# First squares of V in a buffer outside the weights' ring, weight blocks handed out later, and a new planned order

## The chip, the cores and the metric

The kernel runs on one NeuronCore of a Trainium2 chip, as one program of five instruction streams: PE (TensorE, matmuls), DVE (VectorE), ACT (ScalarE), POOL (GpSimd) and SP (SyncE), which here only issues DMAs. The metric is the device time of one execution in microseconds (us). The profile covers one execution; its span runs from the first to the last instruction.

## The reference

Causal attention over 4 batches of 12 heads, 448 positions and 64 dimensions, and behind it a product of four weight matrices on all 1792 tokens.

```python
# _attn_ref(q, k, v), each (4, 12, 448, 64)
scores = scale * np.matmul(q, k.transpose(0, 1, 3, 2))
scores = np.where(mask, -1000000000.0, scores)
scores = scores - np.max(scores, axis=-1, keepdims=True)
attn = np.exp(scores)
attn = attn / (np.sum(attn, axis=-1, keepdims=True) + 1e-09)
return np.matmul(attn, v).astype(np.float32)
...
# _moe_ref(x, w1, w2, w3, w_out), x (1792, 768), d_ff 1024
a = x @ w1
b = x @ w2
h = a * b @ w3
return (h @ w_out).astype(np.float32)
```

The weights arrive as 64-bit numbers. The inputs are random, Q and K enlarged by about 7.5.

## The kernel before

**The steps.** W3 and W_out are multiplied into one matrix first ("w34", line 776, float32, 8 blocks m of 16 products each; W3 is turned on PE in line 764 and the results are evacuated in lines 783 and 784). Attention works on 24 pairs of heads, 6 to a batch. For each pair Q and K are loaded and turned (line 488), the scores are computed (line 571), DVE masks them and takes the maximum (line 588), ACT takes the exponential (line 592), and the probabilities are split into two float16 parts `ph`: the high part on DVE, ACT or POOL (lines 617, 619 and 621), the low part always on DVE (line 624). A transposing DMA brings them into `pt` and `ptt`, PE multiplies them with V (lines 644 and 649), and the result goes into `xt`, again in two parts (lines 658 to 661). The part `pht` (448 columns) is the last one that DVE makes of a pair.

**The gate.** For each batch `gate` multiplies `xt` with 16 weight blocks `w16` (even ones of W1, odd ones of W2; lines 900 to 902, three products for each of 6 pairs of heads d, so 18 to a block). `norms` (line 851) finds the batch's scale before the results can be stored. `project` multiplies the gated values with w34 (lines 960 to 962).

**Weights.** A weight block takes a DMA of 64-bit words, `decode` to float32 (ACT lines 677 and 679, DVE line 681, and the addition of line 684 on POOL or DVE), squares on ACT (line 392) for the scale, a tiny product on PE (line 405), three small DVE instructions (lines 408 to 413), and the two float16 parts (lines 716 to 720 and 723). The float32 values wait in one of three tiles of the ring `da`. A ring hands out its tiles in the order in which the code asks for them, so a user further down the code waits until the user three places earlier is finished with the tile. The squares of V (line 392, called by `take_v`), from which comes the scale of V, use a `da` tile only as a place for unwanted output. In the code `take_v` for batch 0 stands behind all of `w34`, and `w34` with `nf=3` asks for weight blocks 0 to 9 while it goes through m = 3 to 7.

**The order.** The whole program is recorded first as operations with a due time (`Program.add`). `Program.order` is a list scheduler: it simulates the engines with written-down costs and picks, for the engine that is free first, the ready operation with the earliest due time. Where an operation may run on several engines the first free one takes it. The due times come from the table PLAN. The engines then execute their instructions strictly in the recorded order, and SP issues its DMAs in order too.

## Time and profile before

| what | value |
|---|---|
| median of 3 runs | 583.81 us (582.77 to 598.71) |
| profiled execution, its own time | 582.41 us |
| its span, first to last instruction | 580.6 us |
| PE busy | 548.0 us (94% of the span) |
| DVE busy | 383.6 us (66%) |
| ACT busy | 325.2 us (56%) |
| POOL busy | 168.3 us (29%) |
| mean granted TensorE clock | 0.987 |

The table is an average over stages. It is read with a table by stage beside it, in which a stage's length less an engine's busy time is that engine's idle time there, and in which the granted clock tells how much of PE's busy time was spent at half speed.

### The profile page before, as it was taken

The numbers are of one execution on the slowest core, as the hardware profiler recorded it, in microseconds if no ns is written. First come the engines' busy times: TensorE is split into PE (matmuls) and PEld (weight loads), VectorE is DVE, ScalarE is ACT, GpSimd is POOL, SyncE is SP. The second block draws the span as 40 slices with busy tenths as digits, with TensorE's granted clock in tenths as the row PEclk, the third lists the DMA queues.
The fourth block names the chain that finished last, engine by engine and source line by source line (L and its number), as shares of the span: only waits on it lengthen the run. The fifth ranks groups of instructions, "written<-read, shape, count | busy, mean of one in ns | idle before, by whom it ended". The sixth has DMA issues, their size and how long they took to land.

```text
span 580.6 us, 10748 instructions
## 1 busy us (share of the span) xinstructions
PE 548.0 (94%) x3872; PEld 304.4 (52%) x3872; DVE 383.6 (66%) x1057; ACT 325.2 (56%) x764; POOL 168.3 (29%) x128
## 2 busy tenths in 40 slices
PE   3899999886888999999999999999999999999997
PEld 1465555553545555466545555565455566555564
DVE  5635989999897979983587969826897861211100
ACT  6856999877667676853366547534754541111111
POOL 3021674656434445140021533201333410000000
PEclk9999999999889999999999999999999999999999
DMA  8999887798689868676656887786647781000011
GB/s 318 340 255 214 242 206 212 230 198 172 118 162 183 164 145 141 121 147 165 120 112 127 160 145 132 178 193 124 137 94 122 114 175 51 0 1 1 15 42 54
DMA packets 224949, 84.59 MB, mean 146 GB/s; under 512 B 205952, under 2 KB 221824, under 8 KB 224896
## 3 DMA queue, kind: packets, MB, share of 16 engines
q1 hardware_dynamic: 224896, 83.91, 66.4%
q8 instruction: 30, 0.49, 0.4%
q14 instruction: 23, 0.19, 0.1%
HBM read 43.78 MB, written 5.51 MB: 85 GB/s over the span
## 4 chain that ended last, share of the span: by engine, by line
PE 63%; DVE 3%; ACT 1%; DMA 1%; issue 1%; POOL 0%; ACTq 0%; POOLq 0%; DVEq 0%
PE mm L900 8%; PE mm L902 7%; PE mm L901 7%; PE sc L571 6%; PE mm L960 4%; PE mm L962 4%; PE mm L961 4%; PE tr L900 4%; PE tr L901 4%; PE tr L902 4%; PE av L649 3%; PE tr L960 2%; PE tr L962 2%; PE tr L961 2%; PE av L644 1%; DMA qkt<-da 1%
## 5 line engine op out<-in xcount | busy, mean ns | idle before, releaser
L900 PE MATMUL mm<-xt,w 128*128 128x448 f16 x258 | 91.7, 355 | 0.0
L902 PE MATMUL mm<-xt,w 128*128 128x448 f16 x258 | 91.4, 354 | 0.0
L901 PE MATMUL mm<-xt,w 128*128 128x448 f16 x258 | 91.4, 354 | 0.0
L592 ACT ACTIVATE p<-p,mx 128x256 f32<-128x256 f32 (+2 forms) x144 | 71.6, 499 | 23.6 <-DVE mx L588 23.3
L776 PE MATMUL mm<-wof,w3t 128*128 128x384 f32 x192 | 71.1, 513 | 4.9 <-POOL wof L684 2.7
L621 POOL TENSOR_SCALAR ph<-p,rc 128x256 f16<-128x256 f32 (+2 forms) x48 | 47.0, 986 | 87.6 <-DVE rc L602 44.3
L624 DVE SCALAR_TENSOR_TENSOR ph<-p,rc,ph 128x384 f16<-128x384 f32 (+2 forms) x144 | 67.6, 517 | 2.5 <-ACT ph L619 2.2
L571 PE MATMUL sc<-qkt 64*128 64x384 f16 (+7 forms) x480 | 63.2, 365 | 4.0 <-DVE mx L588 3.8
L902 PEld LDWEIGHTS <-w 128*128 128x128 f16 x384 | 37.6, 98 | 40.7 <-issue 5.9
L900 PEld LDWEIGHTS <-w 128*128 128x128 f16 x384 | 37.6, 98 | 39.6 <-issue 7.7
L901 PEld LDWEIGHTS <-w 128*128 128x128 f16 x384 | 37.7, 98 | 31.0 <-issue 1.8
L776 PEld LDWEIGHTS mm<-wof,w3t 128*128 128x128 f32 x192 | 35.5, 197 | 29.7 <-issue 3.6
L960 PE MATMUL mm<-w34h,arena 128*128 128x384 f16 x152 | 49.6, 327 | 0.0
L962 PE MATMUL mm<-w34h,arena 128*128 128x384 f16 x152 | 49.5, 326 | 0.0
L961 PE MATMUL mm<-w34l,arena 128*128 128x384 f16 x152 | 49.5, 326 | 0.0
L901 PE MATMUL tr<-xt,w 128*128 128x448 f16 x126 | 44.6, 354 | 5.1 <-DVE xt L661 5.1
L900 PE MATMUL tr<-xt,w 128*128 128x448 f16 x126 | 44.5, 353 | 0.8 <-ACT at L911 0.5
L902 PE MATMUL tr<-xt,w 128*128 128x448 f16 x126 | 44.6, 354 | 0.0
L422 POOL TENSOR_SCALAR v<-vr,v_s 128x512 f16<-128x512 f32 x15 | 27.1, 1806 | 36.5 <-PE av L649 26.3
L926 ACT CAST arena<-g 128x448 f16<-128x448 f32 x22 | 12.4, 564 | 41.7 <-DVE g L921 41.6
L619 ACT ACTIVATE ph<-p,rc 128x384 f16<-128x384 f32 (+2 forms) x55 | 26.8, 530 | 13.2 <-DVE rc L602 3.7
L588 DVE CUSTOM_DVE_ANT_0 p<-sc,mask,minus 128x384 f32<-128x384 f32 (+2 forms) x72 | 31.5, 476 | 3.2 <-PE sc L571 3.1
(179 smaller groups left out, 1035.9 us busy)
## 6 DMA issues: line engine op xcount, KB each, us to landing
arena<-in_moe_w_dram SPq DMA_DIRECT2D x11, 768.0 KB, 5.0
vr<-in_v_dram SPq DMA_DIRECT2D x24, 192.0 KB, 3.9
out_dram<-osb SPq DMA_DIRECT2D x24, 192.0 KB, 2.1
arena<-in_moe_w_dram SPq DMA_DIRECT2D x8, 512.0 KB, 4.4
xt<-in_moe_w_dram SPq DMA_DIRECT2D x5, 768.0 KB, 6.5
qkr<-in_k_dram SPq DMA_DIRECT2D x12, 224.0 KB, 4.6
qkr<-in_q_dram SPq DMA_DIRECT2D x12, 224.0 KB, 5.7
arena<-in_moe_w_out_dram SPq DMA_DIRECT2D x3, 768.0 KB, 9.5
```

The costliest lines, as they stand in the source:

```text
L571: nc.tensor.matmul(ps[rows if i == 2 else slice(0, P), :w], qs[rows, c * P : c * P + n], ks[rows, 0:w], start=start, stop=stop)
L588: prog.add(due + 0.4, (DVE, t_dve(w) + 0.07, lambda o=o, ps=ps, u=u: nc.vector.tensor_tensor_reduce(out=o, in0=ps[:, :w], in1=m, scale=iv, ...
L592: prog.add(due + 0.9, (ACT, t_act(w, pointers=1, acc=True), lambda o=o, u=u: nc.scalar.activation(out=o, in_=o, func=AF.Exp, scale=-1.0, b ...
L621: (POOL, t_pool(w) + 0.35e-3 * w + 0.16, lambda src=src, r=r, h=h: nc.gpsimd.tensor_scalar(out=h, in0=src, scalar1=r, scalar2=None, op0=AL ...
L624: prog.add(due + 0.4, (DVE, t_dve(w) + 0.06, lambda src=src, r=r, h=h, l=l: nc.vector.scalar_tensor_tensor(out=l, in0=src, scalar=r, in1=h ...
L776: prog.add(due, (PE, 4 * t_mm(NH), lambda: nc.tensor.matmul(ps[:, :NH], w3t[slot(m)][:, g], wof[:, g, ns], start=g == 0, stop=g == KF - 1) ...
L900: nc.tensor.matmul(ps[:, :S], w[:, 0, d], xh, start=d == 0, stop=False)
L901: nc.tensor.matmul(ps[:, :S], w[:, 0, d], xl, start=False, stop=False)
L902: nc.tensor.matmul(ps[:, :S], w[:, 1, d], xh, start=False, stop=d == KD - 1)
L960: nc.tensor.matmul(t, gh[:, fc, cs], w34h[:, fc, ns], start=fc == 0, stop=False)
L961: nc.tensor.matmul(t, gh[:, fc, cs], w34l[:, fc, ns], start=False, stop=False)
L962: nc.tensor.matmul(t, gl[:, fc, cs], w34h[:, fc, ns], start=False, stop=fc == KF - 1)
```

## The change

Three things change in what is computed where, and many in the order. (1) `take_v` for batch 0 writes its unwanted squares into tile 2 of the ring `pt`, no longer into `da`. (2) `wfrom=6` makes `w34` ask for weight blocks 0 and 1 at m = 6 and for 2 and 3 at m = 7; blocks 4 to 15 are asked for behind the first six pairs. (3) PLAN has new numbers throughout; among them `h0` goes from 3 to 0 and `hv` from 5 to 1 (`hold` lets the loads of a pair and of V be issued only behind the decode of the W_out block with that number), and `wfrom=6` and `stick=24.2514` are new. The scheduler also keeps the ready operations of each PE mode apart and prefers the mode that ran last by `stick`, and some of its costs are adjusted. The arithmetic stays the same. In the new file lines from 470 on stand 4 further down, those around 400 stand 2 further down.

```diff
-PLAN = dict(nc=10, wstep=-5.8196, soft=196.756, w0=44.8721, w34=0.3523,
...
+PLAN = dict(nc=10, wstep=3.6064, soft=-6.8718, w0=50.8305, w34=0.7706,
...
-                        heapq.heappush(avail[e], (self.ops[i][0] + late, i))
+                        heapq.heappush(avail[e].setdefault(self.modes.get(i), []), (self.ops[i][0] + late, i))
...
-            if avail[e]:
-                _, i = heapq.heappop(avail[e])
+            tops = [(h[0][0] - (PLAN["stick"] if m == last_mode else 0.0), h[0][1], h) for m, h in avail[e].items() if h]
+            if tops:
+                _, i = heapq.heappop(min(tops, key=lambda x: x[:2])[2])
...
-            (POOL, t_pool(n) + 0.35e-3 * n + 0.16, lambda: nc.gpsimd.tensor_scalar(
+            (POOL, 1.17 * (t_pool(n) + 0.35e-3 * n + 0.16), lambda: nc.gpsimd.tensor_scalar(
...
-        j, jk = da.next()
+        j, jk = da.next() if b else (pt.tiles[2], ("pt", 2))
+        if not b:
+            j = j.rearrange("p t s f -> p (t s f)")[:, : 4 * NP * D]
...
-            for g, c, e in ((POOL, t_pool(n) + 0.01, nc.gpsimd), (DVE, (1.3 * n + 80) / 1000, nc.vector))
+            for g, c, e in ((POOL, t_pool(n) + 0.01, nc.gpsimd), (DVE, (1.04 * n + 78) / 1000, nc.vector))
...
-            for i in range(2 * (m - NF), min(2 * (m - NF) + 2, NC)):
+            for i in range(max(0, 2 * (m - PLAN["wfrom"])), min(2 * (m - PLAN["wfrom"]) + 2, NC)):
                 take_w(i)
...
-        for i in range(min(NC, 2 * (KF - PLAN["nf"])), NW):
+        for i in range(min(NC, 2 * (KF - PLAN["wfrom"])), NW):
             take_w(i)
```

On ACT before, the squares of V (into `da`, their scale goes to `vam`) stand between those of weight blocks 7 and 9 (`w16_7`, `w16_8`, `w16_9`), 131 rows into the program.

```order
L392 ACTIVATE w16_7_116,wam1_133<-da2_108 128x768
L716 ACTIVATE w16_6_115<-da1_107,w_s0_135 128x768
L619 ACTIVATE ph1_93<-p320_88,rc1_151 128x3x128
L677 ACTIVATE da0_106<-arena_104 128x768
L716 ACTIVATE w16_7_116<-da2_108,w_s1_136 128x768
L679 ACTIVATE arena_104<-arena_104 128x768
L677 ACTIVATE da1_107<-arena_104 128x768
L392 ACTIVATE da2_108,vam0_138<-vr0_86 128x1536
L392 ACTIVATE w16_8_117,wam2_134<-da0_106 128x768
```

Now they write `pt2` and stand 29 and 37 rows into ACT's program, among the decodes of W_out, ahead of any weight block.

```order
L596 ACTIVATE p32t0_91,sm0_148<-p32t0_91,mx0_146 128x448
L394 ACTIVATE pt2_97,vam0_138<-vr0_86 128x1536
L496 COPY qkt1_85<-tr0_70 128x448
L496 COPY qkt1_85<-sc3_69 128x448
L681 ACTIVATE da2_108<-w34h_102 128x768
L683 ACTIVATE w34h_102<-w34h_102 128x768
L774 COPY w3t2_124<-tr0_70 128x512
L681 ACTIVATE da0_106<-w34l_103 128x768
L683 ACTIVATE w34l_103<-w34l_103 128x768
L394 ACTIVATE pt2_97,vam0_138<-vr1_87 128x1536
```

So everything that needs the scale of V, above all the first pairs' products with V, is free of the weight blocks.

On DVE before, the sixth pair's last low part (`pht`, line 624, row 327 of DVE's program) comes when the low parts (line 723) of 12 weight blocks stand ahead of it.

```order
L624 SCALAR_TENSOR_TENSOR ph1_93<-p322_90,rc1_151,ph1_93 128x3x128
L624 SCALAR_TENSOR_TENSOR ph1_93<-p322_90,rc1_151,ph1_93 128x2x128
L624 SCALAR_TENSOR_TENSOR ph1_93<-p322_90,rc1_151,ph1_93 128x128
L588 ISA p320_88,mx0_146<-sc3_69,mask_79,minus_81 128x384
L588 ISA mx0_146 128x1
L588 ISA p321_89,mx0_146<-sc0_66,mask_79,minus_81 128x384
L588 ISA mx0_146 128x1
L624 SCALAR_TENSOR_TENSOR pht0_94<-p32t0_91,rc1_151,pht0_94 128x448
```

Now it is row 271, with the low parts of three blocks ahead of it (0, 3 and 2), and the other blocks follow it.

```order
L413 TENSOR_SCALAR inv_105<-inv_105 128x1 x2
L415 RECIPROCAL w_s1_136<-inv_105 128x1
L722 TENSOR_SCALAR w16_1_110<-da2_108,w_s1_136 128x768
L628 SCALAR_TENSOR_TENSOR pht0_94<-p32t0_91,rc1_151,pht0_94 128x448
L727 SCALAR_TENSOR_TENSOR w16_1_110<-da2_108,w_s1_136,w16_1_110 128x768
L410 TENSOR_SCALAR inv_105<-sc1_67 128x1
L415 RECIPROCAL w_s1_136<-inv_105 128x1
L665 SCALAR_TENSOR_TENSOR xt448_100<-av0_63,xt448_100 128x448
```

The attention of batch 0 has moved ahead of nine weight blocks on DVE; the last block's low part (block 15) is now row 410.

On SP before, the W_out blocks (`in_moe_w_out`, 128x1536) are issued close together, with Q and K of one pair among them and V behind them.

```order
L441 DMA w34l_103<-in_moe_w_out_dram 128x1536
L441 DMA w34h_102<-in_moe_w_out_dram 128x1536
L441 DMA arena_104<-in_moe_w_out_dram 128x1536
L441 DMA qkr0_82<-in_k_dram 112x8x64
L441 DMA qkr0_82<-in_q_dram 112x8x64
L441 DMA arena_104<-in_moe_w_out_dram 128x1536
L441 DMA vr0_86<-in_v_dram 128x6x64 x2
```

Now both halves of V and Q and K of two pairs stand between the W_out blocks.

```order
L443 DMA xt512_101<-in_moe_w_out_dram 128x1536
L443 DMA vr0_86<-in_v_dram 128x6x64 x3
L443 DMA vr0_86<-in_v_dram 64x6x64
L443 DMA qkr1_83<-in_k_dram 112x8x64
L443 DMA qkr1_83<-in_q_dram 112x8x64
L443 DMA w34h_102<-in_moe_w_out_dram 128x1536
L443 DMA w34l_103<-in_moe_w_out_dram 128x1536
L443 DMA vr1_87<-in_v_dram 128x6x64 x3
L443 DMA vr1_87<-in_v_dram 64x6x64
L443 DMA arena_104<-in_moe_w_out_dram 128x1536
```

The last four W_out blocks have moved behind the loads of V.

## Rows read from the trace of the kernel before

**Rows 1.** Busy time of each engine by stage (first column: from and to).

```profile
core 0: us, PE busy (x) PEld busy (x) DVE busy (x) ACT busy (x) POOL busy (x), PEclk, DMA share, GB/s
0.00:29.00 29.00, 17.46 (x54) 9.76 (x54) 17.75 (x30) 21.33 (x30) 5.58 (x14) 1.00 0.96 328
29.00:101.60 72.60, 70.97 (x283) 41.02 (x284) 52.48 (x124) 58.13 (x113) 33.73 (x19) 1.00 0.90 226
101.60:188.70 87.10, 73.02 (x560) 41.88 (x559) 78.23 (x223) 64.48 (x164) 45.99 (x31) 0.92 0.89 177
188.70:566.00 377.30, 376.17 (x2916) 205.67 (x2914) 235.16 (x683) 179.50 (x458) 83.03 (x65) 1.00 0.57 112
```

**Rows 2.** PE's waits from 101.6 to 188.7 us: total, times, longest.

```profile
PE tr L901 <- DVE xt L661: 5.1, 1, 5.1
PE sc L571 <- DVE mx L588: 3.8, 4, 1.7
```

**Rows 3.** PE's timeline: start, length, instruction, count, idle time before it.

```profile
106.31 5.33 PE L776 MATMUL mm<-wof,w3t 128*128 128x384 f32 x16
...
144.03 0.53 PE L901 MATMUL tr<-xt,w 128*128 128x448 f16 x1 [5.06 <-DVE xt L661]
...
145.10 0.58 PE L901 MATMUL mm<-xt,w 128*128 128x448 f16 x1
145.47 0.58 PE L902 MATMUL mm<-xt,w 128*128 128x448 f16 x1
...
152.46 0.98 PE L488 MATMUL sc<-ident,qkr 112*128 112x112 f32 x8
...
165.69 1.35 PE L571 MATMUL sc<-qkt 64*128 64x256 f32 x8
...
176.76 0.57 PE L644 MATMUL av<-ptt,v 128*64 128x64 f16 x24 [0.45 <-DMA ptt<-pht]
177.14 1.18 PE L649 MATMUL av<-pt,v 128*64 128x384 f16 x18
```

**Rows 4.** PE by stage, line 900 alone (one of three equal lines), late stretch.

```profile
508.00:522.50 14.50, 9.00 (x26) 2.48 (x26) 1.00 0.01 1
```

**Rows 5.** ACT's timeline, the second of V's squares.

```profile
119.22 1.47 ACT L392 ACTIVATE da<-vr 128x1536 bf16<-128x1536 f32 x1
```

**Rows 6.** DVE's busy time in one stretch, and two rows of its timeline.

```profile
50.70:171.20 120.50, 109.73 (x285) 0.94 0.81 191
...
161.37 0.67 DVE L624 SCALAR_TENSOR_TENSOR pht<-p32t,rc,pht 128x448 f16<-128x448 f32 x1
171.16 0.68 DVE L624 SCALAR_TENSOR_TENSOR pht<-p32t,rc,pht 128x448 f16<-128x448 f32 x1
```

**Rows 7.** DVE's instructions by line and shape: busy us, mean ns of one.

```profile
L723 DVE SCALAR_TENSOR_TENSOR w<-da,w_s,w 128x768 f16<-128x768 f32 x16 | 16.9, 1059 | 2.2 <-POOL w L720 1.9 <-ACT w L716 0.2
L681 DVE TENSOR_SCALAR da<-da 128x768 int32<-128x768 int32 x24 | 14.8, 616 | 8.6 <-ACT da L677 8.5
L718 DVE TENSOR_SCALAR w<-da,w_s 128x768 f16<-128x768 f32 x4 | 3.6, 892 | 0.1
L493 DVE COPY qkt<-sc 128x448 f32<-128x448 f32 x7 | 4.3, 612 | 2.8 <-PE sc L488 2.8
L420 DVE TENSOR_SCALAR w34h<-xt,w_s 128x768 f16<-128x768 f32 x1 | 0.6, 622 | 0.1
L411 DVE TENSOR_SCALAR inv<-inv 128x1 f32<-128x1 f32 x24 | 3.5, 152 | 0.2
```

**Rows 8.** SP's timeline, the first half of V.

```profile
24.66 3.42 SPq L441 DMA_DIRECT2D vr<-in_v_dram  x2
...
29.21 3.00 SPq L441 DMA_DIRECT2D vr<-in_v_dram  x2
```

**Rows 9.** POOL's and DVE's timelines near 219.5 us.

```profile
219.53 1.84 POOL L684 TENSOR_TENSOR da<-da,arena 128x768 int32<-128x768 int32 x1 [2.43 <-issue]
...
219.58 2.28 DVE L624 SCALAR_TENSOR_TENSOR pht<-p32t,rc,pht 128x448 f16<-128x448 f32 x1
```

More of the change, by code (lines that the diff above doesn't have):

```diff
@@ L26 @@
 PE, ACT, DVE, POOL, SP = "PE", "ACT", "DVE", "POOL", "SP"
[L27 removed]
+PLAN = dict(nc=10, wstep=3.6064, soft=-6.8718, w0=50.8305, w34=0.7706, ab=1.9504, out=0.6632, gap=-1.6322, lat=44.2335, begin=-91.0074, wlead=70.5419, urgent=-469.9817, flex=370.3401, sc=-41.0893, vo=-494.4237, av=-194.2706, x=-353.7633, qlead=-514.025, rlead=417.269, v0=250.3178, v1=137.6978, gram=2, nf=3, h0=0, hv=1, ns=7, wo0=372.2276, wo1=301.1492, wom=91.9573, w3a=767.9653, w3l=46.2422, wd=-104.1576, wh=-132.8946, wl=1.1959, fin=-10.7242, ev=483.517, po=[7.835, -22.3194, -46.2642, -45.7187, -46.1544, -168.5123, 44.732, 118.2718, -2.1469, -154.505, -36.8352, 4.8443, 45.9944, -62.3407, -59.3789, -141.4965, -13.9926, -146.366, -84.3586, -180.0751, 32.2385, 37.7583, 62.9194, 45.468], wo=[94.042, -8.263, -88.9315, -217.7217, 115.6771, 99.8526, 211.7957, -24.8481], w3=[-158.8005, -50.8167, -61.9442, -32.663, -51.9857, -143.9432, 16.037, 208.3012], tw=[-214.4914, 58.2404, 21.4694, -22.4979, -112.6908, -172.2348, -114.743, -134.9378, -53.1451, -19.9257, -4.9187, -20.2346, -61.9799, -199.5703, -107.2525, -134.2498], slack=0.1918, pflex=136.6935, fq=2, hlead=80.6809, stick=24.2514, wfrom=6)
 HOP = {
@@ L108, in order @@
         soon = {e: [] for e in free}
-        avail = {e: [] for e in free}
+        avail = {e: {} for e in free}
         ran = [None] * n
-        dma_free, last_mode, lock_end, port_end = 0.0, "full", 0.0, 0.0
+        dma_free, last_mode, lock_end, port_end = 0.0, None, 0.0, 0.0
         edge, busy, warm = PHASE, 0.0, False
@@ L146, in order @@
                         late = PLAN.get({DVE: "flex", POOL: "pflex"}.get(e), 0.0) if self.ops[i][1][0][0] != e else 0.0
-                        heapq.heappush(avail[e], (self.ops[i][0] + late, i))
-                while avail[e] and done[avail[e][0][1]]:
-                    heapq.heappop(avail[e])
-                if avail[e]:
+                        heapq.heappush(avail[e].setdefault(self.modes.get(i), []), (self.ops[i][0] + late, i))
+                for h in avail[e].values():
+                    while h and done[h[0][1]]:
+                        heapq.heappop(h)
+                if any(avail[e].values()):
                     t = free[e]
@@ L195, in order @@
                 if e == PE and cost:
-                    mode = self.modes.get(i, "full")
+                    mode = self.modes.get(i)
                     if mode != last_mode:
@@ L600, in inverse @@
                 out=rc[:, n], in0=sm[:, n], scalar1=1e-9, scalar2=1 / UP, op0=ALU.add, op1=ALU.mult)),
-                [smk + u for u in uk], [rck + u for u in uk])
+                [smk + u for u in uk], [rck + u for u in uk], port=True)
             prog.add(due, (DVE, 0.1, lambda: nc.vector.reciprocal(out=rc[:, n], in_=rc[:, n])), [rck + u for u in uk], [rck + u for u in uk])
@@ L620, in soft @@
                         out=h, in_=src, func=AF.Copy, scale=r)),
-                    (POOL, t_pool(w) + 0.35e-3 * w + 0.16, lambda src=src, r=r, h=h: nc.gpsimd.tensor_scalar(
+                    (POOL, 1.1 * (t_pool(w) + 0.35e-3 * w + 0.16), lambda src=src, r=r, h=h: nc.gpsimd.tensor_scalar(
                         out=h, in0=src, scalar1=r, scalar2=None, op0=ALU.mult)),
@@ L719, in take_w @@
                 out=w16[i][:, 0], in0=tc2, scalar1=s, scalar2=None, op0=ALU.mult)),
-            (POOL, t_pool(DM) + 0.35e-3 * DM + 0.16, lambda: nc.gpsimd.tensor_scalar(
+            (POOL, 1.17 * (t_pool(DM) + 0.35e-3 * DM + 0.16), lambda: nc.gpsimd.tensor_scalar(
                 out=w16[i][:, 0], in0=tc2, scalar1=s, scalar2=None, op0=ALU.mult)),
```

2 lines of the change are left out of this document (removed).

## The prediction

> **What bounds the kernel now.** I read the table by stage first: where is PE idle or slow? From 188.7 to 566.0 us PE is busy for 376.2 of 377.3 us at the full clock [rows 1]. No order can take more than 1 us out of these 377. From 29.0 to 101.6 us it idles 1.6 us [rows 1]. Two stretches are left. In the first 29 us PE idles 11.5 us, while the DMA engines are at 0.96 of their time [rows 1]: the program waits for its first weights. From 101.6 to 188.7 us PE idles 87.1 − 73.0 = 14.1 us, and its granted clock is 0.92 of full speed [rows 1], which costs another 0.08 × 87.1 = 7.0 us of full-speed work. So 21.1 us are lost in one stretch of 87, and it is the only large loss that is not at the program's ends.
>
> The waits of this stretch say who is late: the longest is 5.1 us for `xt` from DVE, then 3.8 us for DVE's maxima, which must leave a score bank before PE can use it again [rows 2]. In PE's timeline the clock follows the wait: after 5.06 us of waiting at 144.03 the products of the gate start 0.37 us apart [rows 3], where the late stretch takes 14.5 / (3 × 26) = 0.186 us for each [rows 4]. That is the 1.2 GHz level for the 2.4 GHz one. DVE meanwhile is busy for 78.2 of 87.1 us [rows 1], and for 109.7 of 120.5 us from 50.7 to 171.2 [rows 6]. **DVE is the bound there**: each microsecond of its work takes 120.5 / 109.7 = 1.10 us.
>
> Why is DVE late? Before the sixth pair's last part `pht` (ending at 171.16 + 0.68 = 171.84 us [rows 6]) it makes 12 weight blocks, of which PE needs only the first few by then. And the pairs could not go first: the scale of V needs the two squares on ACT, of which the second ends at 119.22 + 1.47 = 120.7 us [rows 5], since they stand in the ring `da` behind weight blocks 0 to 7.
>
> **The change part by part.**
>
> *Squares of V into `pt`.* This adds nothing. It frees the products with V from the ring: the squares now stand among the decodes of W_out. By itself it saves the wait of the first pairs only if DVE makes their parts early too, which the new order does; I count the two together.
>
> *Weight blocks later.* From the two orders, ahead of the sixth `pht` DVE has 9 fewer low parts of weight blocks (12 to 3) at 1.06 us, 7 fewer shifts of 768 (20 to 13) at 0.62, 25 fewer of the small scale steps (63 to 38) at 0.15, 4 fewer copies of Q and K (5 to 1) at 0.61 and 2 fewer high parts (4 to 2) at 0.89; against it 3 more high parts of w34 (1 to 4) at 0.62 [rows 7]. That is 9.5 + 4.3 + 3.8 + 2.4 + 1.8 − 1.9 = 19.9 us; smaller differences are left out. Times 1.10 the sixth `pht` ends 21.9 us earlier, at 149.9. From its end to the sixth product with V the trace has 176.76 − 171.84 = 4.9 us, PE's wait being for the transposing DMA [rows 3, 6]. So DVE allows this product at **154.8 us**.
>
> What does PE allow? It started at 176.76 [rows 3]. Without the stretch's losses, of which some 20 of the 21.1 us lie ahead of it (an estimate: the waits behind it up to 188.7 are short), that would be 156.8. PE's order has 16 fewer transposes of Q and K ahead of it at 0.98 / 8 = 0.12 us and 8 fewer score products at 1.35 / 4 = 0.34 (an order row is two records), and 6 more gate products at 0.186 [rows 3, 4]: −1.9 − 2.7 + 1.1 = −3.5. So **153.3 us**: the two limits are 1.5 us apart. The wait in the middle goes, and with it the slow clock.
>
> *What is late next:* the weight blocks, now made while the gate of batch 0 runs. In PE's new order stand, between the sixth product with V and the first product of the last block, 225 gate products at 0.186 (41.9 us), 20 score products at 0.34 (6.8), 32 transposes at 0.12 (3.9), one value set at 0.57 + 1.18 − 0.19 of overlap (1.6) and norms and small rows of about 2 [rows 3, 4]: 56 us. Added to 154.8, PE wants the last block at **211 us**. On DVE stand between the sixth `pht` and the last low part 13 low parts (13.8 us), 11 shifts (6.8), 2 high parts (1.8) and 40 small steps (6.1) [rows 7], in sum 28.5; then the work of 1.3 to 2 pairs at 171.16 − 161.37 = 9.8 us a pair [rows 6], 13 to 20; 6 gate products, counted like a copy of the same shape at 0.61 [rows 7], 3.7; and some 15 single instructions that I bound by 7 and 9. That is 52 to 61 us, times 1.10 57 to 67: the last block is ready at 149.9 + 57 = **207** to **217 us**. So PE waits between 0 and 6 us here in all. I take 4, nearer the upper end, because blocks that arrive just in time leave small waits.
>
> *V, Q and K ahead of W_out.* The first half of V kept SP's queue for 3.42 + 3.00 = 6.4 us [rows 8]; ahead of the last W_out blocks now stand two such halves and the loads of two pairs. DMA is full there (0.96 [rows 1]), so each load that is moved forward delays what stands behind it. The last W_out blocks come later by between 6.4 us (one half) and 13 (two). Does PE starve? Six products wait for each W_out block, 2 records of 5.33 / 16 = 0.33 us each [rows 3], so 4 us of work to a block; of eight blocks the last four are delayed. The work that PE has from the earlier ones (16 us and more) covers the delay, if it is not consumed before. I bound the loss by 0 and 6.4, and take 2: nearest to it is the row of 29 to 101.6 us, where PE idled 1.6 us with the same loads in its neighbourhood [rows 1]. Queued behind on SP are the remaining W3 blocks, whose products come after all of these.
>
> *The rest.* `stick` and the costs move only who takes what. In the whole program DVE has as many instructions as before and POOL ten fewer, so no engine's total becomes a bound. From the gate of batch 1 on PE was never late and has the same work; I cost it at nothing, with DVE's idle time as cover (377.3 − 235.2 = 142 us from 188.7 on [rows 1]).
>
> *The sum*, against the profiled execution of 582.4 us: −21.1 + 4 + 2 = −15.1, so **567 us**. The execution lies 1.4 us under the median of 583.8; I leave that aside. Two per cent, about what a measurement of this kernel can tell from no change, is 11.7 us, so "faster" begins at 572.
>
> **The rivals.**
>
> *Nothing waits.* Both allowances are zero: 582.4 − 21.1 = **561 us**. For it: the limits at the sixth product differ by 1.5 us only. Against it: any single late block in an order without slack.
>
> *DVE and POOL block each other, and the new bound is the weight blocks.* The addition in `decode` on POOL started at 219.53 and took 1.84 us; the `pht` that DVE started at 219.58 took 2.28 us [rows 9], where a free one took 0.68 [rows 6]: 1.6 us lost by being second. In the new order POOL makes this addition for 14 of the 16 blocks, before for 10; and 12 of them are made while DVE is what PE waits for. If half of these twelve meet a DVE instruction at that price, DVE is 6 × 1.6 = 9.6 us later, PE waits 8 us more, and the time is **575 us**; if all twelve do, 585. The Trainium skill (SBUF — State Buffer, "SBUF: two separate sides") speaks against the change in the same way: GpSimd and VectorE hold a shared port pair as an exclusive lock for a whole instruction, and the second one blocks fully. By that rule alone every meeting costs what is left of the 1.84 us; the trace agrees in the one case shown. Against this rival: the pace of 1.10 was measured with POOL busy beside DVE, so some meetings are in it.
>
> *Slower: the gate of batch 0 runs at the low clock.* If blocks come one by one and PE waits before each, the clock may stay at 1.2 GHz as it did after the wait at 144 us. The 288 gate products would cost 0.37 − 0.186 = 0.184 us more each [rows 3, 4], 53 us if all of them did. It decides from about 40% (115 products, 21 us, the whole gain); at 60% the time is 567 + 32 − 7 (then PE is itself so slow that it hardly waits) = **592 us**. For it: the fall was seen after one wait of 5 us. Against it: a slower PE gives DVE time to get ahead, and full work restored the clock before 188.7 us [rows 1].
>
> *The order does not do what it says:* the squares stand early in ACT's program, but V's loads might land late. They are issued before the fifth W_out block, which the first product cannot precede by much; it would cost the first pairs only, and is inside the 2 us above.
>
> **How the numbers follow.** Forecast 567 us (562 to 571): 0.50. Nothing waits, 561: 0.13. Blocked weight blocks, 575 (571 to 581): 0.29. Low clock, 592: 0.08. Faster by over 2%, below 572: the first two and 0.01 of the third, 0.64; within 2%: 0.28; slower: 0.08. The range leaves out the slow case and the ends of the two beside the forecast: 558 to 580 us.
>
> **What would show it.** Right: in the stage from 101.6 to 188.7 us PE's idle time falls below 6 us and the granted clock is 1.00; the first product with V comes before 85 us, long before the squares' old place at 119.22; the sixth `pht` ends near 150; norms of batch 0 near 158; the first rows of line 960 near 230. V's squares lie before 45 us. Wrong: PE waits for low parts of weight blocks (line 727) during the gate of batch 0, which is the third case; many DVE instructions of twice their length beside POOL's line 688 would confirm its cause; gate products at 0.37 us the fourth. The forecast also falls if PE's idle time before 60 us grows by more than 6 us, since then the loads of V were not free, or if waits appear after 250 us, where I counted none.

## The result and the profile after

The changed kernel takes 556.7 us in the median of four runs (555.8 to 557.7), beside 583.8 us for the kernel before, whose one execution in a slower state (598.7 us) is left out of the comparison: the ratio is 0.954, 95% interval 0.951 to 0.957. The forecast was 567 us, with 558 to 580 as its range: right in direction, 10 us too small. The profiled execution took 555.8 us, of which its span is 554.0, beside 580.6 before: 26.6 us less.

The table by stage of the kernel after (columns as in [rows 1]):

```profile
0.00:29.00 29.00, 18.51 (x67) 11.00 (x68) 15.16 (x27) 20.07 (x31) 5.58 (x14) 1.00 1.03 311
29.00:101.60 72.60, 72.54 (x387) 42.28 (x387) 57.78 (x154) 56.99 (x134) 27.01 (x18) 1.00 0.95 210
101.60:188.70 87.10, 85.63 (x617) 47.98 (x615) 81.56 (x201) 74.58 (x154) 49.93 (x28) 1.00 0.97 221
188.70:539.40 350.70, 350.48 (x2753) 193.23 (x2750) 229.90 (x677) 170.50 (x454) 73.53 (x60) 1.00 0.62 115
```

Read against [rows 1]: in the middle stage PE idles 1.5 us instead of 14.1, at the full clock instead of 0.92. In the first 29 us it idles 1.05 us less, from there to 101.6 us 1.57 less. All of PE's waits of the kernel after (engine, line, tile, releaser: us in total, times, longest):

```profile
PE tr L768 <- DVE arena L688: 6.7, 1, 6.7
PE mm L780 <- POOL wof L688: 2.5, 1, 2.5
PE tr L768 <- ACT w3t L774: 1.4, 2, 0.7
PE mm L906 <- DVE w L727: 1.3, 2, 1.0
PE sc L575 <- DMA qkt<-da: 0.2, 1, 0.2
PE tr L407 <- DVE g L921: 0.2, 1, 0.2
```

The first three are waits for the first weights, before 29 us. What replaced the waits of [rows 2] is 1.3 us for two low parts of weight blocks. The events on which the forecast rested, from the timelines of ACT, DVE and PE of the kernel after:

```profile
25.96 1.47 ACT L394 ACTIVATE pt<-vr 128x1536 bf16<-128x1536 f32 x1
37.02 1.47 ACT L394 ACTIVATE pt<-vr 128x1536 bf16<-128x1536 f32 x1
...
139.27 1.12 DVE L628 SCALAR_TENSOR_TENSOR pht<-p32t,rc,pht 128x448 f16<-128x448 f32 x1
...
75.70 0.57 PE L648 MATMUL av<-ptt,v 128*64 128x64 f16 x24
...
148.73 0.57 PE L648 MATMUL av<-ptt,v 128*64 128x64 f16 x24
```

The second square of V is done at 38.5 us instead of 120.7 [rows 5], the sixth `pht` ends at 140.4 instead of 171.84 [rows 6] (forecast 149.9), and the sixth value set (the products of one pair with V) starts at 148.7 instead of 176.76 [rows 3] (forecast 153 to 155).

DVE's busy time from the start to the end of the sixth `pht`, in the kernel before and in the kernel after (from and to, length, DVE's busy time, clock, DMA):

```profile
0.00:171.84 171.84, 134.56 (x330) 0.96 0.88 223
...
0.00:140.39 140.39, 108.32 (x274) 1.00 0.98 236
```

DVE is busy for 26.2 us less ahead of that date, where the forecast counted 19.9.

### The profile page after: what moved, and what is told of

Same layout as the page of the kernel before. It is cut to its first block, busy times and chain, and to the rows that moved or that the text cites. A ratio compares the mean times of both kernels' runs of the same rounds, so it can differ in the third digit from the quotient of the medians.

```text
span 554.0 us, 10756 instructions
## 1 busy us (share of the span) xinstructions
PE 537.5 (97%) x3872; PEld 300.5 (54%) x3872; DVE 384.4 (69%) x1057; ACT 323.9 (58%) x774; POOL 156.1 (28%) x118
## 4 chain that ended last, share of the span: by engine, by line
PE 82%; DVE 9%; ACT 3%; DMA 3%; issue 1%; POOL 1%; POOLq 0%; ACTq 0%
PE sc L575 8%; PE mm L780 8%; PE mm L904 7%; PE mm L905 7%; PE mm L906 7%; PE mm L964 5%; PE mm L966 4%; PE mm L965 4%; PE tr L904 4%; PE av L653 4%; PE tr L905 4%; PE tr L906 4%; PE sc L780 2%; PE tr L964 2%; PE tr L966 2%; PE tr L965 2%
## 5 line engine op out<-in xcount | busy, mean ns | idle before, releaser
L596 ACT ACTIVATE p<-p,mx 128x384 f32<-128x384 f32 (+2 forms) x144 | 71.5, 497 | 28.7 <-DVE mx L592 28.6
L625 POOL TENSOR_SCALAR ph<-p,rc 128x128 f16<-128x128 f32 (+2 forms) x40 | 43.1, 1086 | 69.8 <-DVE rc L606 39.5
L575 PE MATMUL sc<-qkt 64*128 64x384 f16 (+7 forms) x480 | 58.9, 356 | 0.2 <-DMA qkt<-da 0.2
L780 PEld LDWEIGHTS mm<-wof,w3t 128*128 128x128 f32 x192 | 34.2, 193 | 24.3 <-issue 4.1
L592 DVE CUSTOM_DVE_ANT_0 p<-sc,mask,qiv 128x384 f32<-128x384 f32 (+2 forms) x72 | 31.4, 478 | 18.0 <-PE sc L575 17.8
L623 ACT ACTIVATE ph<-p,rc 128x384 f16<-128x384 f32 (+2 forms) x64 | 29.1, 504 | 9.5 <-issue 5.7
L685 DVE TENSOR_SCALAR da<-da 128x768 int32<-128x768 int32 (+1 forms) x38 | 24.2, 639 | 14.9 <-ACT da L681 14.7
```

The source lines that it names most:

```text
L575: nc.tensor.matmul(ps[rows if i == 2 else slice(0, P), :w], qs[rows, c * P : c * P + n], ks[rows, 0:w], start=start, stop=stop)
L592: prog.add(due + 0.4, (DVE, t_dve(w) + 0.07, lambda o=o, ps=ps, u=u: nc.vector.tensor_tensor_reduce(out=o, in0=ps[:, :w], in1=m, scale=iv, ...
L596: prog.add(due + 0.9, (ACT, t_act(w, pointers=1, acc=True), lambda o=o, u=u: nc.scalar.activation(out=o, in_=o, func=AF.Exp, scale=-1.0, b ...
L625: (POOL, 1.1 * (t_pool(w) + 0.35e-3 * w + 0.16), lambda src=src, r=r, h=h: nc.gpsimd.tensor_scalar(out=h, in0=src, scalar1=r, scalar2=None ...
L780: prog.add(due, (PE, 4 * t_mm(NH), lambda: nc.tensor.matmul(ps[:, :NH], w3t[slot(m)][:, g], wof[:, g, ns], start=g == 0, stop=g == KF - 1) ...
```

## The experiments

My theory (the prediction's): the time goes by the work that DVE has ahead of the sixth pair's `pht`; where fewer weight blocks stand there, PE doesn't wait. The first rival: the new numbers carry the gain and the two structural parts do nothing; the other: one structural part carries it alone. A first table of all runs; "idle" is PE's idle time, from tables by stage like the one above.

```
kernel                          median us  ratio to before [95%]    idle 29-101.6  idle 101.6-188.7, clock
before                            582-584  1                              1.6        14.1  0.92
after                             556.7    0.954 [0.951, 0.957]           0.1         1.5  1.00
squares back in the ring          597.0    1.025 [1.021, 1.030]           0.0        22.6  0.84
blocks from 3 on                  583.7    1.000 [0.998, 1.003]           5.0        11.2  0.90
both undone                       611.9    1.051 [1.045, 1.057]           3.3        29.1  0.82
before + squares in pt            595.8    1.023 [1.020, 1.025]           8.3        17.0  0.92
before + blocks from 6 on         584.3    1.003 [1.001, 1.004]          10.9         5.5  0.92
before + both                     600.3    1.031 [1.028, 1.035]           5.4        19.8  0.82
after's code, old numbers         601.5    1.033 [1.029, 1.037]           7.0        20.5  0.86
after, old costs                  571.2    0.980 [0.975, 0.986]           4.3         2.4  0.98
after, no preference of a mode    559.9    0.961 [0.957, 0.966]           0.1         2.1  1.00
after, loads behind W_out         584.3    1.001 [0.999, 1.004]           3.6        12.3  0.90
after, additions on DVE           572.5    0.981 [0.978, 0.984]           5.0         4.2  0.98
before + filler (one execution)   579.3    -                              1.8        10.8  0.98
after + DVE work early            580.9    0.996 [0.994, 0.998]           8.0         9.5  0.98
after + DVE work late             576.5    0.989 [0.984, 0.994]           0.0         0.6  1.00
before, lighter DVE               581.8    0.997 [0.995, 1.000]           1.3        13.9  0.92
before, lighter ACT               581.8    0.998 [0.996, 1.000]           2.4        14.7  0.96
ring, numbers refitted            572.2    0.981 [0.979, 0.982]           3.9         3.8  0.96
blocks from 3, numbers refitted   566.3    0.970 [0.967, 0.972]           6.3         0.1  1.00
```

### A part undone or done alone, the numbers left as they were

In each of these the planner makes a new order for the whole program.

The squares back in the ring:

```diff
-        j, jk = da.next() if b else (pt.tiles[2], ("pt", 2))
-        if not b:
-            j = j.rearrange("p t s f -> p (t s f)")[:, : 4 * NP * D]
+        j, jk = da.next()
```

> The changed kernel with the squares of V of batch 0 back in the ring da, all numbers new. The products with V come after W3 again (128 of W3's output products ahead of the first, 69 in the changed kernel) and 9 low parts stand ahead of the sixth pht (3 in the changed one). My theory: 6 more blocks with their shifts and steps cost DVE some 13 us times 1.06 ahead of the sixth pair, so PE idles 7 to 15 us between 101.6 and 188.7 us, the clock falls again, and the time is 566 to 580 us. The rival, that the new numbers alone carry the gain: 555 to 560 us.

597.0 us: worse than the kernel before, 17 us beyond my upper end.

Weight blocks from block 3 on, and then both parts undone (this and the edit above):

```diff
-wfrom=6
+wfrom=3
```

> The changed kernel with weight blocks handed out from W3 block 3 on as before (wfrom=3), the squares still in pt. The order keeps the pairs first by itself: 2 low parts stand ahead of the sixth pht (3 in the changed kernel), but the last low part is made 27 DVE instructions later (row 437, 410 in the changed one), and no gate product stands ahead of the sixth product with V. My theory (the time goes by DVE's work ahead of the sixth pair): no loss in the pairs; 556 to 563 us, the upper end if the later blocks make PE wait in the gate of batch 0. The rival, that handing the blocks out later is a part of the gain that nothing else gives: 566 to 578 us.

> The changed kernel with both structural parts undone (squares in the ring da, blocks from W3 block 3 on), numbers, costs and the rule on PE's modes new. 12 low parts stand ahead of the sixth pht as in the kernel before. My theory: the stall of the middle stage is back, 9 to 18 us of PE's idle time between 101.6 and 188.7 us and a granted clock below 0.97, 572 to 588 us. The rival, that the numbers alone carry the gain: 555 to 562 us.

583.7 and 611.9 us, both above every range that I gave. The first has 2 low parts ahead of the sixth `pht`, which ends at 135.2 us, earlier than in the changed kernel; still it takes 27 us more, since PE waits elsewhere (3.5 us for `xt` in W3's products, 3.4 for maxima, 2.8 for a weight block's squares on ACT) and is at the low clock behind the waits. That speaks against my theory as it stood: the date of the sixth pair doesn't set the time by itself.

The kernel before with the squares in `pt`, with blocks from 6 on, with both, and with all of the changed code but the old table:

```diff
-        j, jk = da.next()
+        j, jk = da.next() if b else (pt.tiles[2], ("pt", 2))
...
-            for i in range(2 * (m - NF), min(2 * (m - NF) + 2, NC)):
+            for i in range(max(0, 2 * (m - 6)), min(2 * (m - 6) + 2, NC)):
```

> The kernel before, with only the two squares of V of batch 0 moved from the ring da to the third tile of pt. By my theory the time goes by what DVE has ahead of the sixth pair's pht: here 14 low parts of weight blocks (12 in the kernel before, 3 in the changed one), so PE still waits and idles between 101.6 and 188.7 us: 12 to 20 us of idle there, the granted clock below 0.97, 580 to 592 us. By the rival that the squares' place is what held the value products back, the first product with V comes far earlier (before 90 us, at 125.4 before), the middle stage loses at most 8 us, and the time is 560 to 572 us.

> The kernel before with weight blocks handed out from W3 block 6 on and nothing else. 7 low parts ahead of the sixth pht (12), the products with V after 93 of W3's output products (123). My theory: DVE has 5 blocks less ahead of the sixth pair, some 11 us times 1.10, so the stage from 101.6 to 188.7 us gives back about half of its 21 us: 570 to 578 us, less if the last blocks (row 468) then come late. The rival, that blocks handed out later only move the wait to the gate of batch 0: 580 to 588 us.

> The kernel before with both structural parts (squares of V of batch 0 in pt, weight blocks handed out from W3 block 6 on instead of 3), with the old table of numbers and the old scheduler. 12 low parts still stand ahead of the sixth pht on DVE. My theory: no gain to speak of, 576 to 590 us, with 9 us or more of PE's idle time left between 101.6 and 188.7 us. The rival, that the two structural parts make the gain and the numbers only polish it: 555 to 566 us.

> The changed kernel's whole code (squares in pt, blocks from 6 on, the rule that prefers the running PE mode, the new costs for POOL and DVE) with the old table of numbers. 12 low parts stand ahead of the sixth pht. My theory: 575 to 590 us, as with both structural parts alone, since the order of DVE's work decides. Rival one (structure and scheduler make the gain): 555 to 566. If the 3.5 us that PE's busy time lost at an equal clock come from the rule on PE's modes, this kernel is 2 to 4 us faster than the one with the two structural parts alone; if not, within 1.5 us of it beside what DVE's order explains.

595.8, 584.3, 600.3 and 601.5 us. At the old table the rival of a gain from one part alone falls, and the one of a gain from both falls too: without the new table the parts cost up to 19 us. But they don't bear out my theory either, since all lie 4 to 12 us above the upper end that it gave. The 584.3 us of the blocks alone lie in the range of that run's rival, but PE doesn't wait there for a low part of a weight block: its waits are for squares of weight blocks on ACT (7.0 us) and for maxima (7.8). What the runs show is one thing: **numbers that were fitted to other code make an order with waits in new places**, whichever part is undone. So undoing a part measures the misfit together with the part.

### The planner's rules, the loads, and POOL

Four edits of the changed kernel, a run each: no preference of the running PE mode, the old costs for POOL and DVE (the factors 1.17 and 1.1 on POOL taken out again, and DVE's addition back at 1.3 n + 80 ns), V's, Q's and K's loads behind W_out's, and the decode addition on DVE alone:

```diff
-stick=24.2514
+stick=0.0
...
-h0=0, hv=1
+h0=3, hv=5
...
-            for g, c, e in ((POOL, t_pool(n) + 0.01, nc.gpsimd), (DVE, (1.04 * n + 78) / 1000, nc.vector))
+            for g, c, e in ((DVE, (1.04 * n + 78) / 1000, nc.vector),)
```

> The changed kernel with stick=0: the scheduler no longer prefers work of the running PE mode. DVE's landmarks are the same (3 low parts ahead of the sixth pht). If the 3.5 us that PE's busy time lost at an equal clock come from PE's mode order, this kernel takes 558 to 561 us with no more idle time on PE; if they have another cause, 555.5 to 558 us.

> The changed kernel with the planner's old costs for POOL and for the decode addition on DVE. 1 low part ahead of the sixth pht (3), the last at row 420 (410), 15 gate products ahead of the sixth product with V (45). My theory: DVE's order is as good, 555 to 560 us. If the new costs matter by themselves (POOL taken for too fast, work given to it that comes late), 560 to 570 us, with PE's waits for decodes or high parts (lines 688, 724) to show for it.

> The changed kernel with the loads of V, Q and K placed behind those of W_out as in the kernel before (h0=3, hv=5). It tests the allowance of +2 us that I gave to the early loads. By that allowance PE's idle time before 101.6 us would fall by 1 to 3 us here and the time would be 553 to 556 us. By the other reading, that the early loads cost nothing and give PE work earlier, PE idles as much or 1 to 4 us more before 101.6 us, and the time is 556 to 561 us.

> The changed kernel with the addition in the decodes on DVE alone (POOL has 14 of the 16 for the weight blocks in the changed kernel). It tests the third case of the prediction, DVE and POOL blocking each other. If each such addition on POOL held DVE up by 1.6 us, DVE gains about as much as the additions cost it (each some 0.9 us on DVE) and PE's waits stay: 554 to 558 us with DVE's stretched instructions gone. If POOL's additions cost DVE little, DVE has more work ahead of the sixth pair and in the gate of batch 0, and PE waits: 558 to 566 us.

The preference is worth 3.2 us at a table that was fitted with it. The row of busy times of the run without it (the page's first part) shows where most of it lies: PE is busy for 541.7 us, where the kernel after has 537.5, at the same clock.

```profile
PE 541.7 (97%) x3872; PEld 300.4 (54%) x3872; DVE 388.4 (69%) x1061; ACT 322.0 (58%) x768; POOL 160.4 (29%) x120
```

The old costs cost 14.5 us, the later loads 27.6, the additions on DVE 15.8, each more than the longest time that I had allowed. None is small, and again PE's waits lie in several places (in the run with later loads 11.0 us for squares of weight blocks on ACT). The allowance of +2 us for early loads isn't borne out: without them PE idles 3.6 us from 29 to 101.6 us, where the changed kernel idles 0.1. Whether POOL's additions hold DVE up can't be read from the run without them, for the misfit is in it.

### Does the clock follow the wait?

The kernel before, with 40 products of zeros in the wait of 5.06 us:

```diff
+                    if b == 0 and i == 0 and d == 1:
+                        for _ in range(40):
+                            nc.tensor.matmul(ps[:, : 2 * P], ones, mask[:, : 2 * P], start=False, stop=False)
```

> The kernel before with 40 matmuls that add zeros, in the same bank, set between the first two products of the gate at which PE waited 5.06 us for the second xt. It computes the same. It tests whether the low clock of 144 to 160 us follows the wait. If it does, the products behind start 0.19 us apart instead of 0.37, the granted clock of the stage is 0.96 or more instead of 0.92, and the span shrinks by up to 4 us, less what DVE then makes PE wait. If the clock is low for another reason, the products stay 0.37 us apart and the span is 582 to 586 us.

579.3 us in one execution, a span of 577.3 beside 580.6. PE's timeline of this kernel (start, us, engine, line, tile; idle time ahead):

```profile
139.20 4.53 PE L903 MATMUL tr<-mask,ones 128*128 128x256 bf16 x40
144.44 0.35 PE L904 MATMUL tr<-xt,w 128*128 128x448 f16 x1 [0.71 <-DVE xt L661]
144.63 0.35 PE L905 MATMUL tr<-xt,w 128*128 128x448 f16 x1
144.82 0.35 PE L900 MATMUL mm<-xt,w 128*128 128x448 f16 x1
```

The products behind the wait stand 0.19 us apart, not 0.37 [rows 3]: at 2.4 GHz, not 1.2. The low clock does follow the wait, as the forecast had it. And the sixth `pht` ends at 169.2 us instead of 171.84: DVE had itself been late by PE's slow spell.

This spell is the longest of three in the middle stage of the kernel before. They show what the clock cost there (PE's busy time in each, then the granted clock):

```profile
115.50:118.90 3.40, 3.12 (x5) 0.50 1.15 289
142.80:149.70 6.90, 5.67 (x19) 0.51 0.91 153
159.90:163.30 3.40, 3.40 (x22) 0.50 0.84 171
```

PE was busy at half speed for 12.2 us, so the clock cost 6.1 us of work, not the 7.0 that the prediction took from the mean clock of the whole stage.

### The order held fixed

These runs leave every instruction in its row and change only how long some take. In the kernel after, DVE gets an instruction whose result nothing reads behind each of 42 maxima, those of batch 0 (below) or, in a second run, of batch 2 (`2 * NP <= p < 3 * NP`):

```diff
+                    if p < NP:
+                        nc.vector.scalar_tensor_tensor(
+                            out=spent, in0=mask_t, scalar=minus, in1=mask_t, op0=ALU.mult, op1=ALU.subtract)
```

> The changed kernel with its order held fixed: the same instructions in the same rows on each engine, but behind each of the 42 maxima of batch 0's six pairs DVE also reads mask_t twice and writes 448 columns of a tile that nothing reads (some 0.5 us each, 20 to 23 us in all, all ahead of the sixth pht). My theory: the sixth pht, which ends at 140.4 us in the changed kernel, ends 20 to 25 us later, PE idles 15 us or more between 101.6 and 188.7 us, the low clock returns, and the time is 570 to 588 us: what the change gained is given back. If DVE's work there has slack that the profile hides, 557 to 563 us.

> The same 42 additions on DVE, in the changed kernel with its order held fixed, behind the maxima of the pairs of batch 2 instead of batch 0, where DVE has idle time. My theory: 556 to 559 us, since DVE isn't what PE waits for there. If it is DVE's total that counts and not its place, as much as with the additions in batch 0: 570 us and more.

580.9 and 576.5 us. An addition took longer than I had reckoned. The groups by line (busy us, mean ns of one), first of the early run:

```profile
L598 DVE SCALAR_TENSOR_TENSOR spent<-mask_t,minus 128x448 f16<-128x448 bf16 x42 | 33.5, 798 | 0.0
```

The same of the late run:

```profile
L598 DVE SCALAR_TENSOR_TENSOR spent<-mask_t,minus 128x448 f16<-128x448 bf16 x42 | 29.6, 704 | 0.0
```

The stretch of the late additions, from the table by stage of the late run (PE, PEld, DVE, ACT, POOL, clock):

```profile
256.50:362.10 105.60, 92.81 (x733) 49.55 (x728) 95.38 (x257) 56.42 (x151) 23.48 (x20) 0.98 0.60 116
```

And of the kernel after:

```profile
256.50:362.10 105.60, 105.38 (x917) 58.06 (x910) 81.35 (x244) 58.77 (x162) 28.33 (x23) 1.00 0.79 148
```

Early, 33.5 us of work cost 24.2 us (the sixth `pht` ends at 167.4 instead of 140.4). The time is what my theory said; the place is so only in part, since PE idles 8.0 us ahead of 101.6 us and 9.5 behind it, where I expected 15 or more. Late, 29.6 us cost 19.8, where I expected nothing. In that stretch of the kernel after DVE idles 105.6 − 81.4 = 24.2 us and PE only 0.2; with the additions PE idles 12.8 us. **DVE's idle time there was little cover**: of the 29.6 us it took up some 10. Its longest waits there in the kernel after are for scores from PE (10.9 us) and for ACT's part of `xt` (8.0). An addition stands directly behind a maximum, ahead of what the same pair needs next from DVE. Whether another place in DVE's order would have held the work at less cost wasn't tried.

The opposite test, in the kernel before: a lighter DVE, and in another run a lighter ACT.

```diff
+        n = 1 if i < 11 or i == 13 else KD
...
-            out=w16[i][:, 1], in0=tc2, scalar=s, in1=w16[i][:, 0], op0=ALU.mult, op1=ALU.subtract)),
+            out=w16[i][:, 1, :n], in0=tc2[:, :n], scalar=s, in1=w16[i][:, 0, :n], op0=ALU.mult, op1=ALU.subtract)),
```

> The kernel before with its order held fixed, but the 12 low parts of weight blocks that DVE makes ahead of the sixth pht are made for 128 of their 768 columns alone (the other columns keep what the squares left there, so the gate's values are wrong): 12 times 0.8, some 9.6 us less work for DVE at 1.0 to 1.1 us each, nothing else changed. My theory: the sixth pht ends some 10 us earlier, PE's idle time between 101.6 and 188.7 us falls from 14 to about 6 us, and the time is 568 to 575 us. If the loss has another cause than DVE's work ahead of the pairs (the squares' place, loads, the order on PE), 579 to 584 us.

```diff
-        squares(am, t32, lambda: w16[i][:, 1].rearrange("p c f -> p (c f)").bitcast(BF16), DM, T + 4, tk + w5, [ak, ("w16l", i)])
+        cut = P if i < 10 else DM
+        squares(am, t32[:, :cut], lambda: w16[i][:, 1].rearrange("p c f -> p (c f)").bitcast(BF16)[:, :cut], DM, T + 4, tk + w5, [ak, ("w16l", i)])
```

> The kernel before with its order held fixed, but ACT's squares of the first ten weight blocks read 128 of 768 columns (so their scales come from a sixth of the block): ten times 0.85 less some 0.3, about 5 us less work for ACT ahead of the second square of V, which starts at 119.22 us there. The run with a lighter DVE left that place and the time as they were, and DVE only waited more. If ACT, busy for 56.3 of 61 us from 60 to 121 us, is what holds the squares of V back, they start 3 to 5 us earlier and the time is 576 to 580 us. If the two engines and PE hold one another in turn, so that none alone is the bound, the time stays within 2 us of the kernel before.

581.8 us both, 1 to 2 us under the kernel before, as the last case of each forecast had it. The run with the lighter DVE: its low parts, from the groups by line from 50 to 172 us:

```profile
L724 DVE SCALAR_TENSOR_TENSOR w<-da,w_s,w 128x128 f16<-128x128 f32 x12 | 4.5, 375 | 0.7 <-ACT w L717 0.6
```

and the second square of V and the sixth `pht` in its ACT and DVE timelines:

```profile
119.25 1.47 ACT L392 ACTIVATE da<-vr 128x1536 bf16<-128x1536 f32 x1
...
171.03 0.67 DVE L624 SCALAR_TENSOR_TENSOR pht<-p32t,rc,pht 128x448 f16<-128x448 f32 x1
```

The run with the lighter ACT: its squares of weight blocks, from the groups by line from 50 to 121 us:

```profile
L392 ACT ACTIVATE w<-da 128x128 bf16<-128x128 f32 x10 | 3.1, 308 | 1.5 <-POOL da L684 0.9 <-DVE da L684 0.6
```

and its ACT timeline ahead of the second square of V:

```profile
119.70 0.91 ACT L679 ACTIVATE arena<-arena 128x768 int32<-128x768 uint32 x1 [1.05 <-DMA arena<-in_moe_w_dram]
...
120.80 1.47 ACT L392 ACTIVATE da<-vr 128x1536 bf16<-128x1536 f32 x1
```

In the kernel before these twelve low parts took 1.056 us each and these ten squares 0.845. So DVE had 12 × (1.056 − 0.375) = 8.2 us less to do, ACT 10 × (0.845 − 0.308) = 5.4. The square, at 119.22 us before [rows 5], comes at 119.25 and 120.80. The saved time is waited away: ACT waits for a weight block's words (6.4 us in all from 60 to 121 us, 2.8 in the kernel before), and the queue that loads them waits, among others, for POOL. The longest waits of SP's queue in the kernel before from 60 to 121 us:

```profile
SPq L441 <- PE sc L488: 9.1, 2, 4.8
SPq L441 <- POOL da L684: 8.0, 3, 4.7
SPq L441 <- POOL arena L684: 7.9, 3, 4.8
```

The busy times of the kernel before ahead of the second square and behind it (columns as in [rows 1]):

```profile
60.00:121.00 61.00, 57.05 (x224) 32.85 (x226) 55.35 (x136) 56.31 (x113) 37.88 (x21) 0.97 0.83 226
121.00:172.00 51.00, 41.40 (x366) 23.29 (x366) 46.80 (x133) 33.83 (x93) 28.89 (x19) 0.90 0.81 150
```

So neither DVE's nor ACT's work alone paces the kernel before ahead of 121 us. A reading that fits these rows is that load, decode, shift, addition and the release of the slot hand one another on, and that V's squares stand in ACT's queue in that round. It isn't shown: a run with more slots wasn't tried, and neither was one with less work for PE, which is busy for 57.1 of these 61 us and for which SP's queue waits longest. Behind 121 us the question is open too: DVE is busy for 46.8 of 51 us there, and only three of the twelve shortened low parts, some 2 us, lie there.

The Trainium skill (Perfetto Trace Analysis, "Identifying the Most-Contended Engine") says to find the engine with the highest occupancy and to optimize that first; TensorE it judges by other measures than the busy time of its products. Of the others ACT and DVE lead in this stretch with 56.3 and 55.4 of 61 us, and taking 5.4 or 8.2 us off either moved the time by less than 2 us; here the measurement decides against it. Its section "Optimization Strategy" says that where the most contended engine changes over time, interleaving those regimes may help. No run here tests that: in both kernels weight blocks and pairs are interleaved, in different orders.

### The numbers fitted anew

Two kernels undo one part each and get a table of numbers fitted to their own code, by a random search over the planner's own reckoning of the end.

> The changed kernel with the squares of V of batch 0 back in the ring da, and the table of numbers fitted anew to that code (by a random search over the planner's own reckoning of the end, 90 minutes long; the search may have missed a better one). The same part undone with the old fit of the numbers took 597 us. If that loss came from the squares' place, the refit takes 585 us or more; if it came from numbers that no longer fitted, the refit comes near the changed kernel, 557 to 562 us. My theory now is in between: the squares' place is worth something by itself since the products with V can't come before the ring lets the squares through (first value set after 100 us, 75.7 in the changed kernel), but most can be planned around: 564 to 576 us.

> The changed kernel with weight blocks handed out from W3 block 3 on as before, squares in pt, and the table fitted anew to that code by the same search. With the old fit it took 583.7 us. If handing the blocks out later is a part of the gain that nothing else gives, 575 us or more; if the loss was misfit, 557 to 562. My theory: a smaller part than the squares' place, 560 to 569 us, with PE waits for ACT's and DVE's weight work left between 101.6 and 188.7 us.

572.2 and 566.3 us, both in the range of my second theory. With fitted numbers the squares' place is worth 15.4 us and the later handing out 9.6, as far as this search went; a longer one could make both smaller. V's squares in ACT's timeline of the kernel with the ring:

```profile
89.93 1.47 ACT L394 ACTIVATE da<-vr 128x1536 bf16<-128x1536 f32 x1
...
97.73 1.48 ACT L394 ACTIVATE da<-vr 128x1536 bf16<-128x1536 f32 x1
```

Its table by stage:

```profile
29.00:101.60 72.60, 68.66 (x272) 38.89 (x271) 51.99 (x131) 51.91 (x113) 25.41 (x16) 0.95 0.87 212
101.60:188.70 87.10, 83.27 (x660) 46.44 (x660) 79.61 (x215) 67.79 (x159) 45.73 (x31) 0.96 0.88 182
```

Through the ring the squares come at 90 and 98 us, not at 26 and 37, and the first product with V at 103.1 us, not at 75.7. PE idles 3.9 us from 29 to 101.6 us (clock 0.95) and loses 3.8 us and 4% of the clock behind it. How much of this comes from the squares' date isn't shown. With blocks from 3 on the squares come at 38 and 44 us, and PE idles 6.3 us from 29 to 101.6 us all the same and 0.1 behind it, though I had expected its waits there.

## Why the prediction was wrong in its size

**What held.** The loss of the middle stage was the largest, and nearly all of it came back: 12.6 of 14.1 us of idle time, and the clock. The clock followed the wait, as the filler run shows. The first product with V comes at 75.7 us (forecast: before 85), the norms at 153 (158), the first row of line 960, now 964, at 214 (230), and no wait over 0.2 us came behind 250 us. The third case (DVE and POOL) and the fourth (low clock in the gate) didn't come: PE waits 1.3 us for weight blocks, and the gate ran at 1.00. The Trainium skill's lock on the shared ports (SBUF — State Buffer, "SBUF: two separate sides") is in the trace of after, though: a low part of a weight block that usually takes 1.0 us took 2.60 from 170.11 us, beside a POOL addition that had started at 169.79: 1.6 us more, as in [rows 9]. Behind it PE waited 0.3 us for a low part.

**The step that failed in the sum** is the two allowances, "+4" for waits for weight blocks and "+2" for V's loads: PE waited 1.3 us for weight blocks, and the first 101.6 us gave back 2.6 us. Against −15.1 us the span gave −26.6, and the parts add up: the stage recovered 19.6 (12.6 idle and 7.0 for the clock, where 21.1 − 4 = 17.1 was forecast: 2.5 more; the clock at the prediction's price); the first 101.6 us gave 2.6 instead of costing 2 (4.6 more); the rest of the idle time fell by 0.9; and PE's busy time fell by 10.5 us, 548.0 to 537.5, 3.5 more than the 7.0 that I gave to the clock. 2.5 + 4.6 + 0.9 + 3.5 = 11.5. With both allowances at zero, the first rival, I would have said 561, and still missed 5.5 us: the 2.6 of the first 101.6 us, the 0.9 and the 3.5, less 1.5 that PE still idled in the stage.

**The 3.5 us** were in no term. They are rather 4.4, since the clock cost 6.1 us and not 7.0, and their cause is settled in part at most. By the test that I had set they are the preference of PE modes: without it 559.9 us, inside the 558 to 561 of that case. But PE's traces change between full, row, column and quadrant tiles (by the rows and columns of each product) 179 times before, 176 after and 193 times without the preference. If the 4.2 us between the last two are the 17 changes, one costs 0.25 us, and the three between before and after 0.7. Another part is likely that waits read too short: a gate product's row lasts 0.35 us while the next can start 0.19 us after it, so 0.16 us of each wait behind one counts as busy, and the view of PE's waits has 26 before and 8 after. That would be some 3 us, an estimate that no run shows.

**The step that failed in the reason** is "DVE is the bound there: each microsecond of its work takes 1.10 us". It gave the recovered 21.1 us a cause, and a date for the sixth `pht` (149.9; it was 140.4). But 8.2 us less work for DVE at the fixed order of the kernel before moved that `pht` by 0.1 us, to 171.7, where 1.10 for each would have moved it by 9.0. Ahead of 121 us, where nine of the twelve shortened low parts lie, DVE was busy without setting the pace. What did set it there, and whether DVE does behind 121 us, stays open. In the kernel after, the reverse test costs 0.7 us for each us of DVE work, early and late: it is a tight order, in which DVE can't be given more, which isn't the same as that less would help.

**Two counts behind the dates** were off as well. "Smaller differences are left out" left out 6.3 of the 26.2 us by which DVE's work ahead of the sixth `pht` fell; among them are four additions of the decodes, 20 before and 16 after. And "6 more gate products" ahead of the sixth value set isn't so: the traces have 45 in both kernels, so PE's limit would have been 152.2 us, not 153.3; it started at 148.7.

**The cover that wasn't.** "From the gate of batch 1 on ... DVE's idle time as cover (142 us)": I cost the change at nothing there, which came true, but by a wrong reason. 29.6 us of work laid into that cover behind batch 2's maxima cost 19.8.

**"This adds nothing. ... I count the two together"**, of the squares, gave their place no value of its own: with fitted numbers it is worth 15.4 us, the larger of the two parts. That neither part gains at a table fitted to other code is shown by the misfits above; which of the waits each part removes by itself stays open, since any order is a new one.

## What to carry to other kernels

A high busy share doesn't say that an engine sets the pace; shorten some of its instructions at a fixed order, in the stretch that you ask about, and look whether the date that you care for moves. The same test, with added work, tells how much of an engine's idle time is cover at that place. Where a planner's numbers are fitted to the code, undoing a part at the old numbers measures the misfit too: refit, or hold the order fixed. And weigh an allowance for waits against the lower end of its range: both allowances of this sum could have been nothing by their own ranges, and they are the terms that failed.

## What the runs showed of the hardware that I had not expected

A DVE instruction with two bf16 inputs of 448 columns took 704 to 798 ns in the mean, 670 at least, no less than the `pht` of the same width with one float32 and one float16 input (0.68 us [rows 6]): the narrower type saved nothing. A sixth of the columns took ACT's square from 845 to 308 ns and DVE's low part from 1056 to 375, so by an estimate from these two widths, with time growing evenly between them, some 0.2 us of either is there whatever its width.
